# Key sums that stream the values of two heads at once, and extra transposes in other units

## Chip, cores and metric

One core of one Trainium2 chip runs the whole program, in one launch. The metric is the device time in microseconds (us) of one execution. TensorE is called PE below, VectorE DVE, ScalarE ACT, GpSimdE POOL and the queue that issues most DMAs SP, as the profile calls them.

## What is computed

The inputs are fp32. Three stages follow each other: a linear attention with random features over 2 batches of 8 heads, 576 tokens and 64 dimensions, then two mixtures of experts on the 1152 resulting tokens. Only the first stage is touched by the change:

```python
def phi(x):
    proj = np.einsum('bhsd,md->bhsm', x, omega)          # 128 features
    sq = np.sum(x * x, axis=-1, keepdims=True) / 2.0
    h = proj - sq
    h = h - np.max(h, axis=-1, keepdims=True)
    return np.exp(h) / np.sqrt(m)
q_p, k_p = (phi(q_s), phi(k_s))
kv = np.einsum('bhsm,bhsd->bhmd', k_p, v)                # the sums over keys
z = np.sum(k_p, axis=2)
num = np.einsum('bhsm,bhmd->bhsd', q_p, kv)
den = np.einsum('bhsm,bhm->bhs', q_p, z)[..., None] + 1e-06
return (num / den).astype(np.float32)
```

Then `_moe_ref` sums four experts, weighted by given probabilities, and `_moe2_ref` sends each token to one of eight experts.

## The kernel before

The attention is cut into **units**, and each unit goes through stages: `stage_a` transposes its rows of K or Q on PE (tile `tp`) and ACT copies the result out (`xt`, L181); `stage_b` projects on omega on PE (`pj`, L194), then DVE takes the maximum over features (L203), POOL or DVE subtracts and adds the square term (L206, L207, tile `sh`), DVE subtracts it from the projections (L209) and ACT takes the exponential (L210), which leaves the features `phk`, `pht` or `phq`. The squares themselves come from ACT (`sqt`, L168), a DVE reduction (L169) and a small POOL instruction (`sq`, L170).

A unit of K is one head of one head pair of one batch, 512 keys of it. Below, K20 is head pair 2, head 0. Two more units, T0 and T1, hold the last 64 keys of all heads, for heads 0 to 3 and 4 to 7. The order of units in batch 0 is K00, K01, K10, T0, K11, T1, K20, K21, K30, K31; then come Q0 to Q3 (one per head pair), four more units of Q, the units of K and Q of batch 1, and the tails of Q. The last stage of a unit of K is `c`: four matmuls with the features as weights and the values of this head as the moving operand (64 columns and a column of ones: 65), and a fifth for the tail, all summed in one PSUM tile `kvp`, of which DVE copies the 65 columns to `kvall` (L229). The values of both heads of a pair lie in one tile `v`, loaded by two DMAs.

A unit of Q goes on with `c` (transposes of the features, `tpq`), `d` (products with `kvall`, `nm`, and the division on DVE) and `e`.

Each fp32 matmul has two records in the trace, so the ten matmuls of two units of K are twenty records.

The table `WARM` names units by the order of their `stage_a`, from 0: in those the first transpose is made again that many times, into the same place, without effect on the result.

From 17 us on, the weights of the first expert layer come in (`r`, 512 KB each) and are split for it: ACT copies halves to a rounded form (`wf`, L497 and L500) and POOL takes the remainders (L499 and L501). Apart from a few stretches that are written out by hand, a scheduler sets the order of the instructions on each engine when the kernel is built, from costs of its own; on the chip each of ACT, DVE, POOL and SP then works through its list in that order.

Of the kernel before, what the change touches and what calls it, by code (L numbers as in the profile page):

```python
# [18 lines left out]
def perf_moe_kernel(  # L19
# [15 lines left out]
    nc = tc.nc  # L35
    P = 128
    B, H, S, D = q.shape
# [14 lines left out]
    FILL = {20: 1, 22: 1, 27: 3, 31: 2, 32: 1, 33: 1, 35: 1, 41: 1, 43: 1, 45: 1, 47: 1, 51: 2, 53: 1, 55: 1}  # L52
    NEA = 6
    SHV = range(10, 20)
    WARM = {10: 3, 13: 3}
    MS = 2
    XT = 2
    XL = 2
# [53 lines left out]
    def attention(att):  # L112
# [7 lines left out]
        T = {}  # L120
        ps = {}

        def bank(shape, name):
            tag, bufs = "a", 4
            if ps["wide"]:
                tag, bufs = (("a", 4), ("h", 2), ("a", 4), ("o", 2))[ps["n"] % 4]
                ps["n"] += 1
            return (ps["A"] if tag == "a" else psB).tile(shape, F32, tag=tag, bufs=bufs, name=name)
# [36 lines left out]
        def squares(src, name):  # L165
            t = att.tile([P, 8, D], F32, tag="sqt", bufs=1, name="sqt")
            s = att.tile([P, 8, 1], F32, tag="sq", bufs=4, name="sq")
            nc.scalar.activation(t, src, AF.Square)  # L168
            nc.vector.tensor_reduce(s, t, axis=AX.X, op=ALU.add)  # L169
            nc.gpsimd.tensor_scalar(s, s, 0.5 * scale, None, op0=ALU.mult)  # L170
            T["sq", name] = s

        def stage_a(u):
            tp = bank([P, 2 * P], "tp")

            for i in (0,) * WARM.get(ps["u"], 0) + (0, 1):
                nc.tensor.transpose(tp[:, i * P : (i + 1) * P], u["src"](i), ident)  # L177
            ps["u"] += 1
            xt = att.tile([P, 2 * P], F32, tag="xt", bufs=4, name="xt")
            if ps["u"] <= R0:  # L180
                nc.scalar.copy(xt, tp)  # L181
                u["terms"] = ((xt, omBD),)
            else:
                xh = xt.bitcast(F32R)
                xl = att.tile([P, 2 * P], F32R, tag="xl", bufs=XL, name="xl")
                nc.scalar.copy(xh, tp)
                nc.vector.tensor_tensor(xl, tp, xt, op=ALU.subtract)
                u["terms"] = ((xh, omH), (xh, omL), (xl, omH))

        def stage_b(u, tag, bufs):  # L190
            pj = bank([P, 4, M], "pj")
            for i in range(2):
                for n, (x, o) in enumerate(u["terms"]):
                    nc.tensor.matmul(  # L194
                        pj[:, 2 * i : 2 * i + 2, :],
                        x[:, i * P : (i + 1) * P],
                        o,
                        start=(n == 0),
                        stop=(n == len(u["terms"]) - 1),
                    )  # L200
            sh = att.tile([P, 4], F32, tag="sh", bufs=4, name="sh")
            sq = u["sq"]()
            nc.vector.tensor_reduce(sh, pj, axis=AX.X, op=ALU.max)  # L203
            ps["m"] = ps.get("m", -1) + 1
            eng = nc.vector if ps["m"] in SHV else nc.gpsimd
            eng.tensor_tensor(u["shv"](sh), u["shv"](sh), sq, op=ALU.subtract)  # L206
            eng.tensor_tensor(u["shv"](sh), u["shv"](sh), sq, op=ALU.add)  # L207
            ph = att.tile([P, 4, M], F32, tag=tag, bufs=bufs, name=tag)
            nc.vector.tensor_tensor(ph, pj, sh.unsqueeze(2).to_broadcast([P, 4, M]), op=ALU.subtract)  # L209
            nc.scalar.activation(ph, ph, AF.Exp, scale=scale)  # L210
            u["ph"] = ph

        def k_unit(b, hp, h):
            u = dict(
                src=lambda i: T["k", b, hp][:, h, 2 * i : 2 * i + 2, :],
                sq=lambda: T["sq", ("k", b, hp)][:, 4 * h : 4 * h + 4, 0],
                shv=lambda s: s,
            )

            def c():  # L220
                kvp = bank([P, D + 1], "kvp")
                hh = 2 * hp + h
                vt = T["v", b, hp]
                rows = slice(64 * b, 64 * b + 64)
                kpt = T["kpt", hh // 4]
                for j in range(4):
                    nc.tensor.matmul(kvp, u["ph"][:, j, :], vt[:, h, j, :], start=(j == 0), stop=False)  # L227
                nc.tensor.matmul(kvp, kpt[rows, hh % 4, :], T["vt"][rows, hh, :], start=False, stop=True)  # L228
                nc.vector.tensor_copy(kvall[:, b, hh, :], kvp)  # L229

            def a():
                stage_a(u)
                if h == 0:
                    squares(T["k", b, hp].rearrange("p h j d -> p (h j) d"), ("k", b, hp))

            def kb():
                kp = bank([P, 2, M], "kp")
                for i in range(2):
                    nc.tensor.transpose(kp[:, i, :], kvall[:, b, 2 * hp + i, D : D + 1].to_broadcast([P, P]), ident)
                t = att.tile([P, 2, M], F32, tag="kb", bufs=KBB, name=f"kb_{b}_{hp}")  # L240
                nc.scalar.copy(t, kp)
                T["kb", b, hp] = t

            T["mk", b, hp] = kb
            return [a, lambda: stage_b(u, "phk", 5), lambda: None, c]
# [1360 lines left out]
```

## Time and profile before

| | |
|---|---|
| median of three executions | 564.35 us (560.31, 564.35, 569.29) |
| the profiled execution | 565.68 us, its span 564.0 us |
| PE busy | 545.0 us, 97% of the span |
| mean granted clock of PE | 0.987 of 2.4 GHz |
| attention, units of K and Q | to about 136 us |

The span runs from the first to the last instruction; what lies around it is 1.68 us. The granted clock of PE is shown as a share of 2.4 GHz, so that 0.50 is 1.2 GHz. A weight load of PE (PEld) can overlap the matmuls ahead of it.

### The profile page before, as it was taken

How to read it: one execution, taken by the hardware profiler on the slowest of the kernel's cores; microseconds unless marked ns; L12 is line 12 of the kernel's file. 1: busy time of each engine (PE TensorE's matmuls, PEld its weight loads, DVE VectorE, ACT ScalarE, POOL GpSimd, SP SyncE). 2: the span in 40 equal slices, each digit the busy share in tenths (PEclk: the TensorE clock that was granted, in tenths of full speed). 3: DMA queues.
4: the chain of work that ended last, by engine and by line, in shares of the span. 5: the costliest groups of instructions: out<-in, count | busy, mean ns of one | idle time of the engine just before them, and what ended most of it. 6: DMA issues, size and time to landing. Idle time of an engine off the chain costs nothing.

```text
span 564.0 us, 10501 instructions
## 1 busy us (share of the span) xinstructions
PE 545.0 (97%) x4110; PEld 482.6 (86%) x4110; DVE 311.5 (55%) x747; ACT 210.9 (37%) x470; POOL 169.1 (30%) x267
## 2 busy tenths in 40 slices
PE   7898999999999999999999999999999999999894
PEld 5787999887999889999898999898998898888673
DVE  5748877996213368677557678556313314436130
ACT  5558445753112255454444455353112212211100
POOL 3356111102998225334332344003000000113332
PEclk9959999999999999999999999999999999999999
DMA  9945300000000322242222332322002089979910
GB/s 196 276 116 165 113 20 2 0 2 2 1 1 0 129 71 101 85 133 83 74 76 76 103 122 76 136 83 83 0 1 112 2 318 389 328 245 334 369 20 10
DMA packets 53046, 62.76 MB, mean 111 GB/s; under 512 B 15762, under 2 KB 32762, under 8 KB 52992
## 3 DMA queue, kind: packets, MB, share of 16 engines
q1 hardware_dynamic: 50016, 60.34, 32.1%
q0 software_dynamic: 1648, 1.38, 1.2%
q8 instruction: 33, 0.54, 0.4%
q10 hardware_dynamic: 1328, 0.33, 0.3%
q14 instruction: 21, 0.17, 0.1%
HBM read 58.30 MB, written 4.46 MB: 111 GB/s over the span
## 4 chain that ended last, share of the span: by engine, by line
PE 94%; DVE 2%; issue 1%; POOL 1%; DMA 1%; ACT 0%; POOLq 0%; DVEq 0%; ACTq 0%
PE h L512 18%; PE o L533 18%; PE o L691 18%; PE X L634 9%; PE Y L634 7%; PE pj L194 6%; PE kvp L227 3%; PE yps L1351 2%; PE m L1330 2%; PE tp L177 1%; PE gl L989 1%; PE nm L343 1%; PE kvp L228 1%; PE nm L351 1%; PE tpq L314 1%
## 5 line engine op out<-in xcount | busy, mean ns | idle before, releaser
L533 PE MATMUL o<-wf,hhi 128*128 128x512 f32 x288 | 91.8, 399 | 0.0
L691 PE MATMUL o<-w2f,sh 128*128 128x512 f32 x288 | 89.9, 393 | 0.0
L512 PE MATMUL h<-xfar,wf 128*128 128x256 f32 (+1 forms) x480 | 81.4, 310 | 0.0
L512 PEld LDWEIGHTS h<-xfar,wf 128*128 128x128 f32 x480 | 71.9, 188 | 2.7 <-issue 0.4
L523 DVE SCALAR_TENSOR_TENSOR hlo<-h,hhi 128x384 fp32r<-128x384 f32 (+1 forms) x56 | 27.9, 498 | 79.2 <-ACT hhi L522 79.1
L522 ACT ACTIVATE hhi<-h 128x384 fp32r<-128x384 f32 (+1 forms) x56 | 25.0, 446 | 112.5 <-PE h L512 109.0
L533 PEld LDWEIGHTS o<-wf,hhi 128*128 128x128 f32 x288 | 51.5, 189 | 7.5 <-ACT hhi L522 0.3
L533 PE MATMUL o<-wf,hlo 128*128 128x512 f32 x144 | 57.3, 399 | 0.0
L691 PEld LDWEIGHTS o<-w2f,sh 128*128 128x128 f32 x288 | 50.9, 188 | 7.0
L691 PE MATMUL o<-w2f,sl 128*128 128x512 f32 x144 | 56.2, 390 | 0.0
L597 POOL TENSOR_TENSOR sums<-r 128x256 f32<-128x256 f32 x16 | 18.6, 1160 | 110.2 <-DVE ws L610 91.9
L512 PE MATMUL h<-xnear,wf 128*128 128x384 f32 x192 | 37.3, 341 | 0.0
L512 PEld LDWEIGHTS h<-xnear,wf 128*128 128x128 f32 x192 | 33.7, 188 | 1.1
L533 PEld LDWEIGHTS o<-wf,hlo 128*128 128x128 f32 x144 | 27.0, 188 | 6.1 <-DVE hlo L523 0.3
L691 PEld LDWEIGHTS o<-w2f,sl 128*128 128x128 f32 x144 | 27.1, 188 | 6.1
L634 PEld LDWEIGHTS X<-tf,ws 128*128 128x128 f32 x192 | 28.9, 188 | 3.0 <-ACT p L655 0.3
L634 PE MATMUL X<-tf,ws 128*128 128x256 f32 (+1 forms) x192 | 30.8, 295 | 0.0
L1075 POOL TENSOR_SCALAR nmx<-mx 128x1 f32<-128x1 f32 x9 | 2.0, 219 | 93.5 <-DVE act L1001 93.4
L203 DVE TENSOR_REDUCE sh<-pj 128x4 f32<-128x512 f32 x36 | 24.7, 688 | 9.3 <-PE pj L194 9.0
L645 ACT ACTIVATE sh<-p 128x256 fp32r<-128x256 f32 (+1 forms) x32 | 14.2, 444 | 40.1 <-DVE p L669 36.2
L613 DVE TENSOR_TENSOR w2f<-r,w2f 128x1024 fp32r<-128x1024 f32 x16 | 20.8, 1302 | 9.0 <-ACT w2f L611 9.0
L194 PE MATMUL pj<-omBD,xt 128*128 128x256 f32 x72 | 23.6, 468 | 2.1 <-DVE phq L209 1.3
(302 smaller groups left out, 1083.9 us busy)
## 6 DMA issues: line engine op xcount, KB each, us to landing
r<-in_moe_w_dram SPq DMA_DIRECT2D x48, 512.0 KB, 4.4
vw<-in_moe_w_dram SPq DMA_DIRECT2D x20, 1024.0 KB, 9.4
xs_far<-in_moe_w_dram SPq DMA_DIRECT2D x3, 1024.0 KB, 15.0
k<-in_k_dram SPq DMA_DIRECT2D x8, 256.0 KB, 3.5
v<-in_v_dram SPq DMA_DIRECT2D x16, 128.0 KB, 3.2
q<-in_q_dram SPq DMA_DIRECT2D x8, 256.0 KB, 4.3
xrow<-xacc SPq DMA_DIRECT2D x6, 256.0 KB, 5.9
out_dram<-xacc SPq DMA_DIRECT2D x6, 256.0 KB, 5.8
```

The source lines that it names most:

```text
L194: nc.tensor.matmul(pj[:, 2 * i : 2 * i + 2, :], x[:, i * P : (i + 1) * P], o, start=(n == 0), stop=(n == len(u["terms"]) - 1),)
L203: nc.vector.tensor_reduce(sh, pj, axis=AX.X, op=ALU.max)
L227: nc.tensor.matmul(kvp, u["ph"][:, j, :], vt[:, h, j, :], start=(j == 0), stop=False)
L512: nc.tensor.matmul(ph[:, 0:n], wf[:, a, c * P : (c + 1) * P], xx[:, c, :], start=(idx == 0), stop=(idx == 3 * NC - 1),)
L522: nc.scalar.activation(hh[:, 0:n], ph[:, 0:n], AF.Relu)
L523: nc.vector.scalar_tensor_tensor(hl[:, 0:n], ph[:, 0:n], 0.0, hh[:, 0:n].bitcast(F32), op0=ALU.max, op1=ALU.subtract)
L533: lambda idx=idx, a=a, hx=hx: nc.tensor.matmul(outs[t], hx[:, cs], wf[:, a, :], start=(f == 0 and idx == 0), stop=(f == NF - 1 and idx == 2))
L597: G.tensor_tensor(raw(0), quad(1, 0), quad(1, 1), op=ALU.add)
L613: V.tensor_tensor(w2f[:, 1], r2, w2f[:, 0].bitcast(F32), op=ALU.subtract)
L634: nc.tensor.matmul(o, w[a][:, c, :], x[b][:, c, :], start=(start and t == c == 0), stop=(t == 2 and c == 1), skip_group_check=True,)
L645: A.activation(hh[i][:, cs], src, AF.Relu)
L691: nc.tensor.matmul(outs[t], hx[i][:, lo : lo + P], w2f[:, a, i, :], start=(fp == 0 and idx == 0), stop=(fp == NF // 2 - 1 and idx == 5),)
```

## The change

In `c` of a unit of K the moving operand is now the values of both heads of the pair, 130 columns, and PSUM takes a tile of that width; of it DVE copies the 65 columns of this unit's head as before. The other 65 columns are not used. `WARM` changes from three extra transposes in unit 10 (Q0) and three in unit 13 (Q3) to two in unit 9 (K31) and two in unit 13.

```diff
-    WARM = {10: 3, 13: 3}
+    WARM = {9: 2, 13: 2}
...
             def c():
-                kvp = bank([P, D + 1], "kvp")
+                kvw = bank([P, 2, D + 1], "kvp")
+                kvp = kvw[:, h, :]
                 hh = 2 * hp + h
+
                 vt = T["v", b, hp]
                 rows = slice(64 * b, 64 * b + 64)
                 kpt = T["kpt", hh // 4]
                 for j in range(4):
-                    nc.tensor.matmul(kvp, u["ph"][:, j, :], vt[:, h, j, :], start=(j == 0), stop=False)
-                nc.tensor.matmul(kvp, kpt[rows, hh % 4, :], T["vt"][rows, hh, :], start=False, stop=True)
+                    nc.tensor.matmul(kvw, u["ph"][:, j, :], vt[:, :, j, :], start=(j == 0), stop=False)
+                nc.tensor.matmul(
+                    kvw, kpt[rows, hh % 4, :], T["vt"][rows, 2 * hp : 2 * hp + 2, :], start=False, stop=True
+                )
                 nc.vector.tensor_copy(kvall[:, b, hh, :], kvp)
```

The scheduler gives the engines another order with it, from about 14 us of the program to the end of the attention; behind that the lists of all engines are the same as before. Lines below the edit have numbers higher by four. Three places follow.

ACT, from the features of T0 (`pht_186`) to those of K20; the tile `pht_247` holds the features of T1, `xt x2` are K21 and K30, and `wf_0`, `wf_1` are the first weights. Before:

```order
L210 ACTIVATE pht_186<-pht_186 128x512
L181 COPY xt<-tp 128x256
L210 ACTIVATE phk<-phk 128x512
L210 ACTIVATE pht_247<-pht_247 128x512
L181 COPY xt<-tp 128x256 x2
L168 ACTIVATE sqt<-k_3_289 128x512
L497 CAST wf_0_703<-r_0_700 128x512
L497 CAST wf_1_708<-r_0_700 128x512
L168 ACTIVATE sqt<-q_0_359 128x512
L210 ACTIVATE phk<-phk 128x512
```

The same stretch of ACT now:

```order
L210 ACTIVATE pht_186<-pht_186 128x512
L210 ACTIVATE phk<-phk 128x512
L168 ACTIVATE sqt<-k_3_289 128x512
L181 COPY xt<-tp 128x256
L168 ACTIVATE sqt<-q_0_361 128x512
L501 CAST wf_0_701<-r_0_698 128x512
L501 CAST wf_1_706<-r_0_698 128x512
L168 ACTIVATE sqt<-q_1_390 128x512
L210 ACTIVATE pht_247<-pht_247 128x512
L181 COPY xt<-tp 128x256 x2
L504 CAST wf_0_701<-r_0_698 128x512
L168 ACTIVATE sqt<-q_2_419 128x512
```

The two copies of weights and the squares of Q0 and Q1 have moved from behind T1's exponential and the copies `xt` of K21 and K30 to ahead of them.

DVE at the same place, from the maximum of T1 to the features of K20 (the last row). Before:

```order
L203 TENSOR_REDUCE sh<-pj 128x4
L229 COPY kv<-kvp 128x65 x3
L209 TENSOR_TENSOR pht_247<-pj,sh 128x512
L101 TENSOR_REDUCE psm<-praw 128x9
L169 TENSOR_REDUCE sq<-sqt 128x8
L102 TENSOR_SCALAR psm<-psm 128x9
L229 COPY kv<-kvp 128x65
L103 RECIPROCAL psm<-psm 128x9
L203 TENSOR_REDUCE sh<-pj 128x4
L104 TENSOR_TENSOR pn<-praw,psm 128x36
L169 TENSOR_REDUCE sq<-sqt 128x8
L209 TENSOR_TENSOR phk<-pj,sh 128x512
```

The rows of DVE now, between the same two:

```order
L203 TENSOR_REDUCE sh<-pj 128x4
L103 RECIPROCAL psm<-psm 128x9
L169 TENSOR_REDUCE sq<-sqt 128x8
L209 TENSOR_TENSOR pht_247<-pj,sh 128x512
L104 TENSOR_TENSOR pn<-praw,psm 128x36
L233 COPY kv<-kvp 128x65
L203 TENSOR_REDUCE sh<-pj 128x4
L169 TENSOR_REDUCE sq<-sqt 128x8
L209 TENSOR_TENSOR phk<-pj,sh 128x512
```

The square sums of Q1 and Q2 (the two rows of L169) now stand ahead of the subtractions for T1 and for K20.

POOL, around the square term of K31 (the last L206 and L207 of each piece). Before:

```order
L206 TENSOR_TENSOR sh<-sh,sq 128x4
L207 TENSOR_TENSOR sh<-sh,sq 128x4
L170 TENSOR_SCALAR sq<-sq 128x8
L143 MEMSET v_1_776 128x8
L206 TENSOR_TENSOR sh<-sh,sq 128x4
L207 TENSOR_TENSOR sh<-sh,sq 128x4
L501 TENSOR_TENSOR wf_0_703<-r_0_700,wf_0_703 128x512
```

The same place of POOL now:

```order
L170 TENSOR_SCALAR sq<-sq 128x8
L143 MEMSET v_1_774 128x8
L503 TENSOR_TENSOR wf_2_714<-r_1_711,wf_2_714 128x512
L505 TENSOR_TENSOR wf_2_714<-r_1_711,wf_2_714 128x512
L206 TENSOR_TENSOR sh<-sh,sq 128x4
L503 TENSOR_TENSOR wf_3_833<-r_1_711,wf_3_833 128x512
L207 TENSOR_TENSOR sh<-sh,sq 128x4
```

Three remainders of weights now stand ahead of the second of the two small instructions. On SP, the loads of the first K of batch 1 and of the first half of `r` have moved ahead of the two loads of `v_3`, and stand right behind the four loads of Q.

## Rows read from the trace of the kernel before

**Rows 1.** The page: engines' busy time, granted clock in 40 slices, chain by engine.
```profile
PE 545.0 (97%) x4110; PEld 482.6 (86%) x4110; DVE 311.5 (55%) x747; ACT 210.9 (37%) x470; POOL 169.1 (30%) x267
...
PEclk9959999999999999999999999999999999999999
...
PE 94%; DVE 2%; issue 1%; POOL 1%; DMA 1%; ACT 0%; POOLq 0%; DVEq 0%; ACTq 0%
```

**Rows 2.** Stretches: length, busy time and count by engine, clock, DMA share, GB/s.
```profile
14.00:20.00 6.00, 6.00 (x43) 5.33 (x43) 4.74 (x13) 2.44 (x5) 1.36 (x8) 1.00 0.94 272
20.00:26.80 6.80, 5.37 (x33) 4.24 (x31) 4.59 (x9) 4.33 (x10) 3.81 (x9) 1.00 0.98 301
26.80:40.50 13.70, 13.70 (x48) 11.80 (x47) 6.76 (x15) 7.60 (x16) 7.65 (x13) 0.50 0.35 89
40.50:56.00 15.50, 13.61 (x100) 12.04 (x99) 13.53 (x37) 12.66 (x27) 9.41 (x9) 1.00 0.60 193
56.00:100.00 44.00, 44.00 (x334) 41.47 (x333) 34.74 (x98) 21.57 (x50) 7.25 (x27) 1.00 0.14 43
```

**Rows 3.** Timeline of PE: start, length of the run, instruction, idle before.
```profile
20.75 1.99 PE L194 MATMUL pj<-omBD,xt 128*128 128x256 f32 x8 [0.30 <-ACT xt L181]
22.58 0.71 PE L177 MATMUL tp<-ident,q 128*128 128x128 f32 x5
23.96 1.08 PE L227 MATMUL kvp<-v,phk 128*128 128x65 f32 x8 [0.67 <-POOL wf L499]
...
35.13 1.81 PE L227 MATMUL kvp<-v,phk 128*128 128x65 f32 x8
...
40.78 0.60 PE L269 MATMUL tpq<-ident,phq 128*128 128x128 f32 x4
...
42.05 1.10 PE L343 MATMUL nm<-kv,qT 128*128 128x65 f32 x8
42.99 1.08 PE L194 MATMUL pj<-omBD,xt 128*128 128x256 f32 x4
```

**Rows 4.** Timeline of PE's weight loads, for the second `kvp` of rows 3.
```profile
23.93 0.97 PEld L227 LDWEIGHTS kvp<-v,phk 128*128 128x128 f32 x8 [0.88 <-POOL wf L499]
```

**Rows 5.** Timeline of ACT.
```profile
20.32 0.65 ACT L181 COPY xt<-tp 128x256 f32<-128x256 f32 x2 [1.12 <-PE tp L177]
20.86 0.64 ACT L168 ACTIVATE sqt<-k 128x512 f32<-128x512 f32 x1
21.67 1.14 ACT L497 CAST wf<-r 128x512 fp32r<-128x512 f32 x2 [0.17 <-DMA r<-in_moe_w_dram]
...
23.25 0.61 ACT L210 ACTIVATE phk<-phk 128x512 f32<-128x512 f32 x1
```

**Rows 6.** Timeline of DVE.
```profile
21.53 0.69 DVE L169 TENSOR_REDUCE sq<-sqt 128x8 f32<-128x512 f32 x1 [0.69 <-ACT sqt L168]
...
22.73 1.28 DVE L203 TENSOR_REDUCE sh<-pj 128x4 f32<-128x512 f32 x2
25.48 0.69 DVE L209 TENSOR_TENSOR phk<-pj,sh 128x512 f32<-128x512 f32 x1 [1.47 <-POOL sh L207]
```

**Rows 7.** Timeline of POOL.
```profile
22.31 0.23 POOL L170 TENSOR_SCALAR sq<-sq 128x8 f32<-128x8 f32 x1 [0.94 <-DVE sq L169]
22.50 2.50 POOL L499 TENSOR_TENSOR wf<-r,wf 128x512 fp32r<-128x512 f32 x2
24.96 0.21 POOL L206 TENSOR_TENSOR sh<-sh,sq 128x4 f32<-128x4 f32 x1
```

**Rows 8.** Timeline of the DMA queue SP: when issues began, and how long they took.
```profile
11.24 2.00 SPq L149 DMA_DIRECT2D q<-in_q_dram  x4
...
16.13 0.56 SPq L149 DMA_DIRECT2D k<-in_k_dram  x1
16.74 0.47 SPq L486 DMA_DIRECT2D r<-in_moe_w_dram  x1
```

**Rows 9.** The page: DMA issues, KB each, median time to landing.
```profile
r<-in_moe_w_dram SPq DMA_DIRECT2D x48, 512.0 KB, 4.4
```

## Prediction

> **What bounds the kernel now.** I read the page first: PE is busy for 97% of the span and 94% of the chain that ended last is PE, so a change counts by what it does to PE's time: its work, its waits and its clock. The 40 slices of the granted clock show one loss, a slice at half speed near the start [rows 1]. A table by stretches places it: from 26.8 to 40.5 us the clock is 0.50, 1.2 GHz, and PE is busy for all 13.70 us; in the 6.8 us ahead of it the clock was full and PE was busy for only 5.37 us [rows 2]. At half clock PE is the bound: DVE and ACT work for 6.76 and 7.60 us in that stretch. At full clock PE's work there would take some 6.85 us, so 6.85 us is the most that a kept clock could give. From 40.5 to 56 us PE waits for 1.89 us of 15.5, with DVE and ACT busy for 13.53 and 12.66; from 56 to 100 us PE never waits [rows 2].
>
> The change lies in these stretches. Whoever reads the diff alone sees wider matmuls and one transpose more or less; the lists of the engines show that the larger part is a new order, and it has to be costed on ACT, DVE and POOL, which the wide matmuls don't touch.
>
> **Columns.** 160 records (16 units of K, ten records each) stream 130 columns and not 65. Eight records of 65 columns take 1.08 us, 0.135 each, and their eight weight loads 0.97 us, 0.12 each [rows 3, 4]: the load of 128x128 weights sets the pace, not the columns. For 130 columns the trace has no row. The nearest are transposes, of 128 columns: a run of five took 0.71 us and one of four 0.60, so one more costs 0.11 us, no more than a weight load. On the other side four records of 256 columns took 1.08 us, 0.27 each; on a line from 65 to 256 columns a record of 130 gains 0.045 us [rows 3]. The 80 records of batch 0 lie where PE waits anyway; the 80 of batch 1 lie in the stretch where it never does. So 0 to 3.6 us; a saving is excluded, since no instruction becomes shorter. I take 0, by the transposes, which are much the nearest.
>
> The Trainium skill weighs against the change here: TensorE: Matmul & The Clock Gate, section "Back-to-back issue gap", gives the start-to-start time of a warm matmul as its columns divided by 2.4 GHz plus 2.5 ns, by which (an estimate) 65 more columns add 27 ns, 2.2 us for the 80 records, and the sum below would be 569.5. The row of 128 columns speaks for the other reading, and no row of before settles it for 130.
>
> The second head's values are in the same tile, and their DMA was issued right behind the first's; no unit waits longer for them that I can see.
>
> **Transposes.** The three that go from Q0 (0.33 us at 0.11) stood ahead of a `kvp` for which PE then waited 0.67 us [rows 3]: gain 0. The two in K31 stand ahead of another `kvp` that must wait for its features (below): cost 0. One fewer in Q3 is 0.1 us. The sum of these is at most 0.3 us either way; I take 0.
>
> **The new order.** Before, ACT copied `xt` of K21 and K30 at 20.32 us and then, at 21.67, reached the first copy of weights, for which it waited on the DMA [rows 5]. Now that copy, a second one and the squares of Q0 and Q1 stand ahead of the `xt`. When does the first `r` land? It is issued right behind the four loads of Q (11.24 and 2.00 long) and one of K (0.56), at 13.8, not at 16.74 [rows 8]. At the median of 4.4 us to landing [rows 9] it is there at 18.2. But the DMA engines are busy for 94% from 14 to 20 us, at 272 GB/s [rows 2]; what really leaves the queue ahead of it are two loads of V, 256 KB, 0.96 us at that rate, so it lands at 20.7 by that reading. I take 20.0, nearer to the full queue.
>
> From there, at the durations of [rows 5 to 7] (a copy of weights 0.57, squares 0.64, square sum 0.69, maximum 0.64, subtraction 0.69, exponential 0.61, `xt` 0.33, a remainder on POOL 1.25, its two small ones 0.25 each, `sq` 0.23), each step waits for the one ahead of it on its engine or for its data:
>
> First, two copies, squares of Q1, then DVE's square sum, which now stands ahead of T1's subtraction, then that subtraction, T1's exponential and `xt`: 20.0 + 1.14 + 0.64 + 0.69 + 0.69 + 0.61 + 0.33 = 24.1. The projections of K21 and K30 start then, not at 20.75 [rows 3]. Second, the other `xt`, a copy, squares of Q2, their sum on DVE (ahead of K20's subtraction), subtraction, exponential: 24.1 + 0.33 + 0.57 + 0.64 + 0.69 + 0.69 + 0.61 = 27.6 for the `kvp` of K20, before 23.96. Third, from K20's subtraction at 27.0: POOL has `sq` from 26.3, a remainder, K21's two small ones, a remainder and K30's two, to 30.0; K30's subtraction and exponential to 31.3; `xt` of Q0 and squares of Q3 to 32.3; their sum to 33.0; then POOL's `sq`, two remainders, a small one, a third remainder and the other small one of K31: 33.0 + 0.23 + 2.5 + 0.25 + 1.25 + 0.25 = 37.5; subtraction and exponential: 38.8 for the `kvp` of K31, before 35.13 [rows 3]. Fourth, `xt` and squares on ACT, the square sum, four small DVE instructions and a maximum between them, Q0's subtraction and exponential: 38.8 + 0.33 + 0.64 + 0.69 + 0.75 + 0.64 + 0.69 + 0.61 = 43.2 for the first `tpq`, before 40.78.
>
> So the units of K end 2.4 us later, **with full clock throughout**: the 6.85 us that the clock gives back are eaten by new waits, some 3.7 us ahead of 24.1, 1.5 ahead of 27.6 and 3 ahead of 38.8. With the landing at 18.2 or 20.7 it is +0.6 or +3.1.
>
> **The clock.** The row of before shows it falling behind a stretch with 1.4 us of waits in 6.8. The new order has a longer wait, so I expect a fall here too, and perhaps a second one at 38.8. At half clock eight `kvp` records take 1.81 us for 1.08 [rows 3], but most of that lies beside the chain on ACT, DVE and POOL. Bounds: 0, if all is hidden, and 6.85, half of another stretch like the old one. I take 1.5, near the low end, since PE has over 8 us of waits there to hide it.
>
> **What comes back.** Eleven of the sixteen copies of weights now stand ahead of the first `qT` on ACT, before seven: 4 x 0.57 = 2.3 us leave ACT in the next stretch. There PE waits for 1.89 us in all [rows 2], so 0 to 1.9; DVE, the busier one, isn't relieved: I take 1.0.
>
> **Sum.** 565.7 (the profiled execution) + 2.4 + 1.5 - 1.0 = 568.6. That execution was 1.3 us above the median of 564.35, so 567.3, rounded to **567 us**. Own range of this case: 564 to 571, by the landing (-1.8, +0.7), the clock (-1.5, +2.5) and what comes back (-0.9, +1).
>
> **Rivals.** (1) The clock holds, and PE stays the bound: the waits of my chain are shorter than I make them (the landing early, POOL and ACT a little ahead), wide `kvp` keep PE at 2.4 GHz. Then the stretch of 13.7 us shrinks, at best to ACT's 7.60: 565.7 - 6.1 = 559.6, less 1.3: 558. For it: PE had no idle time in that stretch. Against it: the lists above. Chance 0.27.
>
> (2) Slower: the clock falls a second time, at the wait ahead of K31's `kvp`, and stays at 1.2 GHz through the first units of Q for as long as before, 13.7 us. PE is busy for 13.61 of 15.5 us there at full clock, so of the 6.85 us lost only 1.89 find room: +5.0, 573.6 with the rest of my sum less 1.3, 572. It decides as soon as the granted clock reads 0.50 for over 8 us behind 40 us; with a third fall it passes 576. For it: fewer expert matmuls fill PE among the first units of Q now. Against it: these units kept the clock before, with PE waiting for 1.89 us [rows 2]. Chance 0.15.
>
> (3) Columns are paid by their number: + 3.6 us in batch 1, 571. For it the 256 columns of rows 3, against it the transposes. Chance 0.1. The rule of the Trainium skill's section named above (TensorE: Matmul & The Clock Gate, "Back-to-back issue gap") would be this rival at 2.2 us.
>
> **How the numbers follow.** My case 0.48, rival 1 0.27, rival 2 0.15, rival 3 0.1. The executions of before differ by 9 us, so a median of a few is itself uncertain by 2 us or so. Low 557: rival 1, 558, and half of that; high 574: rival 2, 572, and that. Outside lie a part of rival 1 (0.1) and of rival 2 (0.07), under 0.2. A difference under 2% (11.3 us) can hardly be told from none here: faster than 553 would need more than all of the 6.85 us, 0.03; slower than 576 needs rival 2 with more, 0.07; within, 0.9.
>
> **What would show it.** Right: PE waits for over 2 us ahead of the projections of K21; ACT's copy of weights waits on the DMA until about 20 us and stands ahead of `xt`; the first `tpq` at 42 to 45 us; eight `kvp` records of 130 columns still at about 1.08 us; the granted clock 0.50 somewhere from 23 to 31 us. Wrong: the first `tpq` ahead of 40 us and the clock at 1.00 throughout (rival 1); or `kvp` records 0.04 us longer where PE never waits (rival 3). What would upset all of it is the phase of the clock's falls, which the three executions of before, 9 us apart, may already reflect.

## The result, and the profile after

The changed kernel takes **566.49 us** (median of 21 executions, 564.89 to 570.21), the kernel before, beside it on the same chips, 563.60 (21 executions, 558.94 to 569.29). The ratio is 1.0064 with a 95% interval from 1.0042 to 1.0085: no difference at a bound of 2%, a small loss by the interval. The profiled execution took 567.01 us, its span 565.3. The ratios here and below leave out executions more than 1.5% longer than the fastest of the same kernel (three of ten in the run no_split_before below), so they are not the quotients of the medians.

The page of the changed kernel, PE's row and the granted clock in 40 slices:

```profile
PE 542.3 (96%) x4108; PEld 477.9 (85%) x4108; DVE 312.8 (55%) x747; ACT 211.8 (37%) x470; POOL 168.0 (30%) x267
...
PEclk9899999999999999999999999999999999999999
```

Against [rows 1], PE has 2.7 us less work in the trace (less of it at half clock), but the span is 1.3 us longer. The same stretches as in [rows 2], of the changed kernel:

```profile
14.00:20.00 6.00, 6.00 (x43) 5.15 (x42) 5.63 (x14) 3.16 (x6) 1.75 (x10) 1.00 0.99 305
20.00:26.80 6.80, 3.82 (x14) 2.94 (x13) 3.24 (x7) 4.61 (x10) 4.54 (x8) 0.75 1.12 321
26.80:40.50 13.70, 12.29 (x73) 9.66 (x73) 8.55 (x19) 8.64 (x18) 9.41 (x17) 1.00 0.51 142
40.50:56.00 15.50, 13.25 (x100) 11.73 (x99) 13.97 (x37) 11.78 (x25) 8.66 (x8) 1.00 0.52 154
56.00:100.00 44.00, 44.00 (x326) 40.29 (x325) 34.66 (x98) 21.33 (x46) 5.33 (x26) 1.00 0.12 36
```

The stretch at half clock from 26.8 to 40.5 us is gone (0.50 to 1.00): the clock is at 1.2 GHz only from 23.3 to 26.7 us. In its place PE waits, for 2.98 + 1.41 + 2.25 = 6.64 us from 20 to 56 us; in [rows 2] it was 1.43 + 0 + 1.89 = 3.32. Where PE waits, its timeline shows (start, length, instruction, idle before):

```profile
23.86 3.40 PE L194 MATMUL pj<-omBD,xt 128*128 128x256 f32 x8 [2.98 <-ACT xt L181]
...
27.31 1.06 PE L229 MATMUL kvp<-v,phk 128*128 128x130 f32 x8
...
37.17 1.16 PE L229 MATMUL kvp<-v,phk 128*128 128x130 f32 x8 [1.06 <-ACT phk L210]
...
39.92 0.66 PE L273 MATMUL tpq<-ident,phq 128*128 128x128 f32 x4
```

These are the four places of the chain in the prediction (24.1, 27.6, 38.8 and 43.2 there; 20.75, 23.96, 35.13 and 40.78 in [rows 3]). ACT's timeline shows where the first wait comes from:

```profile
21.36 1.14 ACT L501 CAST wf<-r 128x512 fp32r<-128x512 f32 x2 [2.36 <-DMA r<-in_moe_w_dram]
22.41 0.62 ACT L168 ACTIVATE sqt<-q 128x512 f32<-128x512 f32 x1
22.94 0.61 ACT L210 ACTIVATE pht<-pht 128x512 f32<-128x512 f32 x1
23.46 0.62 ACT L181 COPY xt<-tp 128x256 f32<-128x256 f32 x2
```

The copies stand ahead of `xt` and wait 2.36 us for `r`, against 0.17 us in [rows 5], where `xt` had gone ahead of them.

Something that I had not foreseen stands in DVE's timeline, in its small instructions (L206, L207; 128x4 elements), and beside them in POOL's, in the remainders:

```profile
39.16 1.02 DVE L207 TENSOR_TENSOR sh<-sh,sq 128x4 f32<-128x4 f32 x1
...
41.54 1.10 DVE L206 TENSOR_TENSOR sh<-sh,sq 128x4 f32<-128x4 f32 x1
42.68 0.16 DVE L207 TENSOR_TENSOR sh<-sh,sq 128x4 f32<-128x4 f32 x1
...
46.15 1.20 DVE L207 TENSOR_TENSOR sh<-sh,sq 128x4 f32<-128x4 f32 x1
```

```profile
38.90 2.50 POOL L503 TENSOR_TENSOR wf<-r,wf 128x512 fp32r<-128x512 f32 x2 [0.39 <-ACT wf L501]
...
41.36 1.27 POOL L505 TENSOR_TENSOR wf<-r,wf 128x512 fp32r<-128x512 f32 x1
...
46.05 2.63 POOL L503 TENSOR_TENSOR wf<-r,wf 128x512 fp32r<-128x512 f32 x2
```

The one at 42.68 takes 0.16 us with POOL idle; the three others begin just behind the start of a remainder and end with one (40.18 and 40.15; 42.64 and 42.63; 47.35 and, at half of the run's 2.63 us, 47.37). Four of them take over 0.3 us (the fourth, at 45.66, ends with a remainder too), 3.78 us together; from 40.5 to 56 us, where three of them lie, DVE is busier than PE (13.97 us against 13.25).

### The profile page after: what moved, and what is told of

The parts are those of the page before. It is cut to its first block, busy times and chain, and to the rows that moved or that the text cites. A ratio compares the mean times of both kernels' runs of the same rounds, so it can differ in the third digit from the quotient of the medians.

```text
span 565.3 us, 10491 instructions
## 1 busy us (share of the span) xinstructions
PE 542.3 (96%) x4108; PEld 477.9 (85%) x4108; DVE 312.8 (55%) x747; ACT 211.8 (37%) x470; POOL 168.0 (30%) x267
## 3 DMA queue, kind: packets, MB, share of 16 engines
q0 software_dynamic: 1648, 1.38, 1.2%
## 4 chain that ended last, share of the span: by engine, by line
PE 89%; DVE 3%; issue 2%; DMA 2%; POOL 2%; ACT 1%; SPq 0%; POOLq 0%; DVEq 0%
PE h L516 18%; PE o L537 18%; PE o L695 18%; PE X L638 9%; PE Y L638 7%; PE pj L194 4%; PE m L1334 2%; PE yps L1355 2%; PE gl L993 1%; PE kvp L229 1%; DMA r<-in_moe_w_dram 1%; PE tp L177 1%; PE nm L347 1%; PE nm L355 1%; PE tpq L318 1%
## 5 line engine op out<-in xcount | busy, mean ns | idle before, releaser
L516 PE MATMUL h<-xfar,wf 128*128 128x256 f32 (+1 forms) x480 | 80.1, 310 | 0.0
L601 POOL TENSOR_TENSOR sums<-r 128x256 f32<-128x256 f32 x16 | 18.2, 1138 | 111.0 <-DVE ws L614 92.0
L194 PE MATMUL pj<-omBD,xt 128*128 128x256 f32 x72 | 22.4, 447 | 3.6 <-ACT xt L181 3.2
```

The lines of the kernel that those rows point to most:

```text
L194: nc.tensor.matmul(pj[:, 2 * i : 2 * i + 2, :], x[:, i * P : (i + 1) * P], o, start=(n == 0), stop=(n == len(u["terms"]) - 1),)
L516: nc.tensor.matmul(ph[:, 0:n], wf[:, a, c * P : (c + 1) * P], xx[:, c, :], start=(idx == 0), stop=(idx == 3 * NC - 1),)
L601: G.tensor_tensor(raw(0), quad(1, 0), quad(1, 1), op=ALU.add)
```

## The experiments

Twelve runs in four groups; each group has executions of the kernel before on the same chip, the changed kernel itself was timed beside none of them, and so runs are compared by their ratios. No run has the wide sums in the order of before. "Last nm" is the start of the last run of `nm` in the profiled execution, the end of the attention on PE: 135.63 us in the first trace of before, 135.65 in that of after.

| run | us | before, same chip | ratio, 95% interval | first tpq | last nm |
|---|---|---|---|---|---|
| before_again | 564.84 | 565.85 | 0.9994, 0.9963 to 1.0026 | 34.5 | 130.84 |
| wait_filled | 569.85 | 565.85 | 1.0076, 1.0039 to 1.0113 | 39.8 | 135.32 |
| no_transposes | 570.62 | 565.85 | 1.0094, 1.0062 to 1.0125 | 39.4 | 135.11 |
| narrow_new_transposes | 571.77 | 565.85 | 1.0089, 1.0049 to 1.0129 | 41.7 | 137.30 |
| r_early | 569.88 | 565.14 | 1.0103, 1.0061 to 1.0145 | 35.9 | 135.35 |
| r_earlier | 569.20 | 565.14 | 1.0083, 1.0056 to 1.0110 | 39.7 | 136.56 |
| r_early_before | 567.25 | 565.14 | 1.0048, 1.0018 to 1.0079 | 37.2 | 132.06 |
| no_split_dve | 562.73 | 565.14 | 0.9967, 0.9938 to 0.9995 | 36.7 | 130.28 |
| no_split_before | 559.26 | 564.44 | 0.9907, 0.9877 to 0.9938 | 34.6 | 128.89 |
| no_split_early | 562.97 | 564.44 | 0.9971, 0.9949 to 0.9992 | 37.7 | 132.38 |
| write_only_pool | 563.11 | 564.44 | 0.9992, 0.9962 to 1.0023 | 36.9 | 133.67 |
| no_squares_before | 557.11 | 563.61 | 0.9875, 0.9836 to 0.9915 | 34.3 | 126.17 |

My theory at the start, **the order**: the lists of ACT, DVE and POOL, with `r`'s landing at their head, set the time of the changed kernel. Rival, **the clock**: how often PE falls to 1.2 GHz sets it, and waits only feed that.

**The kernel before, again** (no edit).

> The kernel before, unchanged, run against itself. Both theories: ratio 1.000 within 0.4%. What it tells apart is how its executions spread. Order theory: in the order of before PE is the bound between 26.8 and 40.5 us, so an execution is the longer the lower its mean granted clock is: 558 to 560 us at a mean clock of 0.995 and more, 564 to 569 at 0.985 to 0.988; the order of after does not follow its clock like that. Clock theory (the change acts through the clock and the columns alone): the executions of before and of after lie on one line of time against clock.

The median is the same, but the profiled execution isn't: its clock held through the attention (the page's row, and three of its stretches).

```profile
PEclk9999999999999999999999999999999999999998
```

```profile
20.00:26.80 6.80, 4.92 (x28) 3.99 (x28) 4.34 (x10) 4.23 (x10) 3.83 (x9) 1.00 1.01 305
26.80:40.50 13.70, 12.06 (x79) 10.13 (x78) 12.06 (x27) 10.65 (x22) 8.81 (x14) 1.00 0.53 155
40.50:56.00 15.50, 13.98 (x107) 13.04 (x108) 14.11 (x42) 12.68 (x29) 10.46 (x10) 1.00 0.54 156
```

Without the fall PE does 79 instructions from 26.8 to 40.5 us, not 48 [rows 2], and waits for 1.88 + 1.64 + 1.52 = 5.04 us from 20 to 56 us, not 3.32; the first `tpq` comes 6.3 us sooner and the attention ends 4.8 us sooner. So the fall is no property of the order of before: it comes in some executions. The trace I predicted from was one with a fall, and its last `nm` equals that of after by that accident. The mean granted clock of every execution tells how often, though not where in the kernel: of the 34 executions of before beside this group 17 stand at 0.990 or less (median 568.15 us) and 16 at 0.994 or more (562.79). Of the 21 of after none is below 0.991, and their times, 564.89 to 570.21, hardly follow the clock. That is the kind of spread that the theory of the order had, though at 0.995 and more it had before at 558 to 560 us.

**PE's long wait filled with transposes** (in the changed kernel, six more in K30, order otherwise unchanged).

```
-    WARM = {9: 2, 13: 2}
+    WARM = {8: 6, 9: 2, 13: 2}
```

> The changed kernel with six more transposes in the unit ahead of the long wait at 20.9 us (unit 8, K30); the lists of all engines are otherwise the same, row by row. Order theory: the wait ends when ACT's list ends it, at 23.9 us, whatever PE does in it; if the clock no longer falls at 23.3 us, the sums of K20 start at 26.6 and not at 27.3 us, so 0 to 1 us faster than after's 566.5. Clock theory: the fall is what the change costs; without it 2 us or more faster, or, if transposes don't keep the clock, no difference.

The clock no longer fell at 23 us; it fell at 38.0 instead, behind a wait of 1.75 us ahead of K31's `kvp`. The attention ends 0.3 us sooner than in after, and the time is that of the changed kernel within its interval. A clock kept at one wait was lost at a later one.

**No repeated transposes at all** (in the changed kernel).

```
-    WARM = {9: 2, 13: 2}
+    WARM = {}
```

> The changed kernel without any extra transposes; lists otherwise the same, row by row. Order theory: within 0.7 us of after (566.5), since the four transposes that go lay beside waits of PE (the clock may fall once more near 35 to 39 us, mostly beside the chain on ACT, DVE and POOL). Clock theory: the transposes are there for the clock, so a second stretch at half clock appears and costs 1.7 us or more: 568 to 570.

The fall is at 23.45 us as in after, the last `nm` 0.5 us sooner, and the time again that of the changed kernel. The moved transposes do nothing that can be seen here, where the interval is 1.8 us to either side.

**The new transposes alone** (65 columns; in the kernel before).

```
-    WARM = {10: 3, 13: 3}
+    WARM = {9: 2, 13: 2}
```

> The kernel before (65 columns) with only the new table of extra transposes. ACT's list stays that of before up to 28 us: the copies xt of K21 and K30 stand ahead of the weights. Order theory: the projections of K21 start at 20.5 to 21 us as before, and the time is that of before or better, 560 to 565 us, faster than after by 2 to 5 us. Clock theory: with narrow sums the clock falls at least as long as before, 13 us, and the time is 564 us or more.

Among the slowest of the first group, where the theory of the order had it fast. K21's projections stand at 21.07 us as before, but a copy of weights on ACT now stands ahead of K21's features, the clock fell for 10.2 us, and PE waits for 3.56 of the 15.5 us from 40.5. Two fewer transposes make the scheduler write lists that are as bad as those of the 130 columns, with sums of 65. The rival had the time (564 us or more), but from a fall of 13 us or more.

**`r` earlier** (in the changed kernel, loaded with K21; then with K20; then the first of these in the kernel before).

```
-                with_load(ku(2, 1), kl(3), vl(3)),
+                with_load(ku(2, 1), kl(3), vl(3), lambda: load_raw(0, 0)),
```

> The changed kernel with one edit: the first raw weights r are loaded with the loads of the unit K21, ahead of those of Q, and not behind them. Theory of the order (ACT's copies of weights, which now stand ahead of xt, wait for r's landing at 21.3 us, and everything behind follows): r lands at 16 to 18 us, the projections of K21 and K30 start at 20 to 21.5 us and not at 23.9, the first tpq comes 1.5 to 3 us ahead of 39.9, and the time is 2 to 4 us below the changed kernel's, 562 to 565 us on a chip like the first. Theory of the clock (PE's falls set the time, the landing only shifts waits): a fall comes somewhere else and the time is within 1 us of the changed kernel's, 566 to 568. Third way: r takes the place of q's loads in a full queue, q's land 1 us later and Q's units pay it back: 566 to 569.

> As the run above, with r loaded one unit sooner, with the loads of K20. Theory of the order: no further gain over the run above, since r at 15.7 us is there before ACT comes to its copies; 562 to 565 us. If the landing isn't what ACT waits for, both runs equal the changed kernel. If the queue of loads pays for it, this one is 0.5 to 1 us worse than the run above, since 128 KB now stand ahead of K21's loads too.

> The kernel before with the same edit as the first run of this call (65 columns, the old transposes, r loaded with the loads of K21). Theory of the order: in the kernel before ACT waits for r for little (its projections of K21 stand at 20.75 us, ahead of the copies), so an early r moves it by 0 to 1 us either way, 563 to 566 us, and by the new lists (copies ahead of features) perhaps 1 us up. Theory of the clock: what decides is how often the clock falls in the stretch behind 23 us; with PE's waits unchanged the executions stay in two groups some 6 us apart and the median stays where it is.

None is faster, and the theory of the order fails at its own test. In the first, `r` is there at 15.5 us and the first `tpq` comes 4.1 us sooner, but the projections of K21 don't (23.71), and the attention ends only 0.3 us sooner. At 23 us ACT's `xt` now waits for T1's features, which wait for T1's small instructions on POOL, which stand behind four remainders that an early `r` let in: another wait in the place of the one removed. And behind 40 us DVE gives the rest back. PE, DVE and POOL in that run:

```profile
23.71 1.99 PE L194 MATMUL pj<-omBD,xt 128*128 128x256 f32 x8 [1.39 <-ACT xt L181]
...
35.85 0.66 PE L273 MATMUL tpq<-ident,phq 128*128 128x128 f32 x4 [0.20 <-ACT phq L210]
...
52.10 1.13 PE L194 MATMUL pj<-omBD,xt 128*128 128x256 f32 x4 [1.38 <-DVE phq L209]
```

```profile
48.86 1.24 DVE L206 TENSOR_TENSOR sh<-sh,sq 128x4 f32<-128x4 f32 x1
50.14 1.18 DVE L207 TENSOR_TENSOR sh<-sh,sq 128x4 f32<-128x4 f32 x1
51.35 0.69 DVE L209 TENSOR_TENSOR phq<-pj,sh 128x512 f32<-128x512 f32 x1
```

```profile
48.81 2.49 POOL L505 TENSOR_TENSOR wf<-r,wf 128x512 fp32r<-128x512 f32 x2 [0.58 <-ACT wf L504]
```

Two remainders end at 50.05 and 51.30; DVE's two small instructions, 0.3 us of work, end at 50.10 and 51.32, and PE's projections wait 1.38 us for what stands behind them. Six such took 5.58 us in this run. The clock held throughout, so the rival, the clock, doesn't explain it either. In the kernel before an early `r` cost a little.

**A third theory: DVE held by POOL.** Without DVE's two small instructions for the units Q0 to Q3 and the other units on DVE (a rounding step of the shift is left out), in the changed kernel:

```
-            eng.tensor_tensor(u["shv"](sh), u["shv"](sh), sq, op=ALU.subtract)
-            eng.tensor_tensor(u["shv"](sh), u["shv"](sh), sq, op=ALU.add)
+            if ps["m"] not in SHV:
+                eng.tensor_tensor(u["shv"](sh), u["shv"](sh), sq, op=ALU.subtract)
+                eng.tensor_tensor(u["shv"](sh), u["shv"](sh), sq, op=ALU.add)
```

> The changed kernel without the two small DVE instructions (subtract sq and add it back) for those units whose squares go through DVE; this leaves a rounding step out of the features' shift. Theory of the collision (those instructions, some 0.15 us long, took 1.0 to 1.2 us where they lay beside a remainder on POOL, four times between 39 and 46.5 us, 3 us in all, and DVE is the engine that is late there): the stretch from 40 to 56 us gets 1.5 to 3 us shorter and the time falls to 563 to 565 us on a chip like the first. Rival (the long ones only fill waits of DVE, which is late for POOL's sq anyway): only the 0.15 us each of those on the path go, 0 to 0.6 us, 565.5 to 567.

562.73 us, just below the 563 to 565 expected, and PE's waits from 40.5 to 56 us, 2.25 us in after, are gone:

```profile
40.50:56.00 15.50, 15.50 (x124) 14.66 (x123) 13.09 (x33) 11.88 (x28) 8.12 (x7) 1.00 0.62 197
```

The attention ends 5.4 us sooner, more than the 3.8 us that the four long ones took. But 3.25 us of that are won by the first `tpq` (36.67 for 39.92), which waits for a subtraction on DVE (38.43 in after) that stands ahead of the first long one (39.16): that part belongs to the lists, which changed too. From the first `tpq` to the last `nm` it is 93.6 us against 95.7. So this run leaves 2.1 us for the place and doesn't show the mechanism. The next one tests that: all of DVE's small instructions stay, and POOL's remainders become fills that write as many places and read none (the low parts of the first expert layer's weights are left out).

```
-        eng.tensor_tensor(l1, s1, d1.bitcast(F32), op=ALU.subtract)
+        eng.tensor_tensor(l1, s1, d1.bitcast(F32), op=ALU.subtract) if e else eng.memset(wf[:, 1, :].bitcast(F32), 0.0)
...
```

> The changed kernel with POOL's remainders of the first expert layer's weights replaced by a fill with zeros, which writes the same 128x512 places but reads nothing; the low parts of those weights are left out, and POOL no longer waits for ACT's copies. DVE's two small instructions are all there. Theory of the port (DVE's small instruction has two inputs in SBUF, and is held until a POOL instruction that reads SBUF is done): all of them take 0.15 to 0.2 us, also beside a fill, and the waits of PE behind 40 us shrink: 561 to 564 us. Rival (DVE is slowed by any POOL work beside it, or by what waits for its semaphores): some still take 0.5 to 1.2 us and the time stays at 565 to 568.

All occurrences of the two instructions, in the changed kernel and then in this run (count, shortest, median and longest ns, first and last start):

```profile
L206 DVE TENSOR_TENSOR sh<-sh,sq x10: 151/152/1102, 37.6 to 66.8; 128x4 f32<-128x4 f32 x10
L207 DVE TENSOR_TENSOR sh<-sh,sq x10: 150/153/1197, 38.2 to 67.2; 128x4 f32<-128x4 f32 x10
```

```profile
L206 DVE TENSOR_TENSOR sh<-sh,sq x10: 151/152/163, 34.6 to 64.3; 128x4 f32<-128x4 f32 x10
L207 DVE TENSOR_TENSOR sh<-sh,sq x10: 134/161/165, 34.8 to 64.7; 128x4 f32<-128x4 f32 x10
```

The longest is 0.165 us, and two of the twenty lay beside a fill and were over before it was:

```profile
39.86 0.52 POOL L505 MEMSET wf<- 128x512 f32 x1
40.09 0.15 DVE L206 TENSOR_TENSOR sh<-sh,sq 128x4 f32<-128x4 f32 x1
40.31 0.13 DVE L207 TENSOR_TENSOR sh<-sh,sq 128x4 f32<-128x4 f32 x1
```

So, as far as two go, it takes a POOL instruction that reads. A rule of the Trainium skill says what these rows show (SBUF — State Buffer, section "Who interferes with whom"): a VectorE instruction with two inputs in SBUF contends with a GpSimd instruction that reads SBUF, not with one that only writes. The same section of the Trainium skill says that the order of issue decides which of the two is blocked; each of the four long ones in after began behind the POOL instruction that it ended with. L206 and L207 have both inputs in SBUF; the subtraction L209 has one in PSUM, and its 0.69 us are the same everywhere.

The time is another matter. The theory's range of 561 to 564 us holds the 563.11, but not for its reason: PE's waits behind 40 us were to shrink, and they stayed at 2.21 us (2.25 in after):

```profile
40.50:56.00 15.50, 13.29 (x99) 11.96 (x98) 13.41 (x38) 11.87 (x25) 0.70 (x3) 1.00 0.57 169
```

From the first `tpq` to the last `nm` it is 96.7 us here and 95.7 in after. What was won was won ahead of the first `tpq` (36.9 for 39.9 us): the fills are shorter (0.53 us against 1.27), and K31's two small instructions, which stand behind them on POOL, come at 31.8 and 32.4 us and not at 34.2 and 35.5. This run shows what holds DVE's instructions, and not that the holding costs the kernel time.

**The same instructions left out of the kernel before, and with an early `r`** (edits as above).

> The kernel before without DVE's two small instructions for the units whose squares go through DVE (the same rounding step left out as in the run without them on the changed kernel; 65 columns, the old transposes). Theory of the collision (these instructions, when they lie beside a remainder on POOL, make up what tells the two kernels apart once r has landed): with none left in either, the two are within 1 us of each other, here 561 to 564 us on a chip like the last. Rival (the order of before is the better one in itself, since its projections of K21 don't wait for r): 3 us or more below the changed kernel without them, 557 to 560 us. Third way (clock): two groups again, some 6 us apart, the lower one at 557 to 560.

> The changed kernel without DVE's two small instructions and with r loaded with the loads of K21. Theory of the collision (it ate what the early r had won, 4.1 us at the first tpq and 0.3 at the end of the attention): now the early r keeps what it wins, but PE has no wait left behind 40 us, so only PE's wait ahead of K21's projections (2.05 us in the run without the small instructions) can go: 1 to 2 us below that run, 560.5 to 562. Rival (an early r costs elsewhere, in the queue of q's loads): the same as that run or 1 us more, 562.5 to 564.

Two misses of the third theory, which had the two kernels within 1 us of each other. 559.26 us is 3.5 us below the changed kernel without them (0.9907 against 0.9967). Part of the 3.5 is the clock, as their mean clocks show: 20 of the 27 executions of before in this group stand at 0.988 or less, four of the ten of this run, none of the twelve of no_split_dve. Between executions at 0.995 or more this run is 2.1 us below before (558.79 against 560.88) and no_split_dve 0.3 us (562.31 against 562.59).

The profiled executions show where the rest lies. Beside before_again the attention ends 1.95 us sooner, none of it won by the first `tpq` (34.6 for 34.5); from there on it is 94.3 us against 96.4, 2.1 us less, as in the changed kernel (93.6 against 95.7). By these two pairs these instructions, with their own 0.15 us each and with what they were held, cost both kernels about the same behind the first `tpq`, some 2 us; that can hide what an earlier stage wins, but isn't what tells the two apart. That lies ahead of the first `tpq`: 5.4 us between before_again and after, 2.1 between the two runs without these instructions.

And an early `r` again won nothing (562.97); its profiled execution had the clock at 1.2 GHz from 18.2 to 25.0 us.

**The kernel before without square terms** (they cancel but for rounding; squares, sums, small instructions and that rounding are left out).

```
         def squares(src, name):
-            t = att.tile([P, 8, D], F32, tag="sqt", bufs=1, name="sqt")
...
+            pass
...
-            eng.tensor_tensor(u["shv"](sh), u["shv"](sh), sq, op=ALU.subtract)
-            eng.tensor_tensor(u["shv"](sh), u["shv"](sh), sq, op=ALU.add)
```

> The kernel before without the square terms at all: no squares on ACT, no square sums on DVE, no small instructions on DVE or POOL that subtract them from the maximum and add them back (they cancel but for rounding, which is left out). Theory (the chain over ACT, DVE and POOL is what PE waits for ahead of 56 us, some 2.7 us in the run of the kernel before without DVE's small instructions): most of these waits go, 1 to 2.5 us below that run, and an execution at a lower mean clock is rarer since PE waits less; 556 to 558 us on a chip like the last. Rival (the waits are for loads and copies of weights, which stay, and the scheduler's new lists bring others): 558.5 to 562 us.

```profile
20.00:26.80 6.80, 6.50 (x44) 5.63 (x43) 5.02 (x13) 3.87 (x8) 2.61 (x3) 1.00 0.73 227
26.80:40.50 13.70, 13.70 (x97) 12.43 (x96) 9.22 (x21) 10.68 (x24) 8.51 (x9) 1.00 0.77 229
40.50:56.00 15.50, 15.50 (x128) 14.93 (x127) 13.13 (x34) 11.96 (x28) 9.15 (x8) 1.00 0.71 224
```

The fastest of all, 557.11 us, where the theory of the chain had 556 to 558, and the steadiest (556.40 to 558.13): PE waits for 0.3 us from 20 to 56, and no execution's mean clock is below 0.996.

## Why the prediction was right, and where its steps failed

The time (567 for 566.49) and "no difference" were right, and most of the picture: PE waits ahead of K21's projections for the landing of `r`, one fall of the clock in 23 to 31 us, the gain from the old fall eaten by waits. Several sizes were wrong and cancelled, and that the time agrees to 0.5 us is luck in good part.

**Columns: taken as 0, measured 0.86 us in batch 1 and up to 1.7 in all.** At full clock, where PE never waits, a `kvp` of batch 1 in after, and one in the second trace of before:

```profile
74.48 1.06 PE L229 MATMUL kvp<-v,phk 128*128 128x130 f32 x8
75.47 0.49 PE L230 MATMUL kvp<-vt,pht 64*128 64x130 f32 x2
75.88 0.39 PE L194 MATMUL pj<-omH,xt 128*128 128x256 f32 x1
```

```profile
70.22 1.00 PE L227 MATMUL kvp<-v,phk 128*128 128x65 f32 x8
71.16 0.43 PE L228 MATMUL kvp<-vt,pht 64*128 64x65 f32 x2
71.52 0.39 PE L194 MATMUL pj<-omH,xt 128*128 128x256 f32 x1
```

From the first start to that of the next work it is 1.40 us against 1.30. Over the eight units of batch 1, from unrounded starts, the price is 0.054 us for the eight records and 0.054 for the two: 0.108 us a unit, 0.86 us for batch 1 and as much for batch 0 where PE is not waiting. It comes once per run of records and not per record, so the weight load does set the pace within a run, as I argued, and rival 3's 3.6 us are out. The formula that I weighed there (the Trainium skill, TensorE: Matmul & The Clock Gate, "Back-to-back issue gap") would make it 2.2 us in batch 1, an estimate; the trace gives 0.86. The same section says that the formula is a lone matmul's and that in a stream of weight loads and matmuls both set the pace, and that part the trace bears out.

**Transposes: 0, right.** Without any, or with six more, the time stays within the intervals.

**The new order: +2.4, measured -0.9 at the first `tpq`.** Of the four places 24.1 and 27.6 were met (23.86, 27.31), the first by two errors that cancel: `r` landed at 21.3 us, not 20.0, and the square sum of Q1, which I put ahead of T1's subtraction, ran behind it (23.07): the sum that stands ahead is Q0's, and both were done by 20.3, before `r` came. The two sums that I called Q1's and Q2's when I listed DVE's rows are thus Q0's and Q1's. The second place was met by luck too: K20's features were done at 26.6 us, and PE, at half clock until 26.7, came to them at 27.3.

```profile
19.04 0.69 DVE L169 TENSOR_REDUCE sq<-sqt 128x8 f32<-128x512 f32 x1 [0.17 <-ACT sqt L168]
19.64 0.68 DVE L209 TENSOR_TENSOR pht<-pj,sh 128x512 f32<-128x512 f32 x1
...
23.07 0.69 DVE L169 TENSOR_REDUCE sq<-sqt 128x8 f32<-128x512 f32 x1 [1.90 <-ACT sqt L168]
...
29.65 0.68 DVE L169 TENSOR_REDUCE sq<-sqt 128x8 f32<-128x512 f32 x1
...
36.97 0.67 DVE L169 TENSOR_REDUCE sq<-sqt 128x8 f32<-128x512 f32 x1
```

The step that failed is the last two: 38.8 was 37.17, and 43.2 was 39.92. In the third I let POOL wait for Q3's square sum, to 33.0 us; the one that it waits for is again a unit earlier, Q2's, done at 30.3, and 0.99 us of waiting for ACT's copies took back a part. In the fourth I put Q0's square sum, maximum and small steps behind K31's exponential; on the chip a square sum (36.97) and the maxima (36.37, 37.63) ran beside it or right behind. I had called a first `tpq` of 42 to 45 us the sign of my case; at 39.92 it came just ahead of the 40 us that I named for rival 1, whose other half, a held clock, didn't come.

**The clock: +1.5, measured 1.4.** PE was busy for 2.87 us of the 3.4 at 1.2 GHz, half of which is lost. What I missed is the base: I read the 13.65 us at half clock as part of the kernel, and it is part of some executions. The second fall of rival 2 didn't come: from 26.8 us on the stretches of after stand at 1.00.

**What comes back: -1.0, wrong in sign.** PE's waits from 40.5 to 56 us grew from 1.89 to 2.25 us. I asked only how much ACT was relieved; three of the four waits in that stretch, 1.64 of the 2.25 us, are for DVE, whose instructions were held beside POOL there.

The account of the two profiled executions: waits 6.64 - 3.32 = +3.3; half clock (13.65 - 2.87) / 2 = -5.4; columns +1.7; two transposes fewer, 0.11 each, -0.2. That makes -0.6, where the layer behind the attention ends 0.4 us later; a remainder of about 1 us I can't place. The last 0.9 us of the 1.3 come behind 514 us, where the change has no part that I know of.

Against the second trace of before, in which the clock held, the same account makes +1.6 for waits, +1.4 for the clock and +1.5 for columns and transposes: 4.5 of the 4.8 us between the ends of the attention. So the change costs some 4.8 us against an execution of before whose clock holds, and nothing there against one whose clock falls; the medians, 2.9 us apart, lie between. The 3.5 us between the two kernels without DVE's small instructions are made in the same way: 1.8 us are left between executions at a mean clock of 0.995 or more, and 1.4 between the ends of the attention in their profiled ones. What stays open is what decides, in an execution of one and the same kernel, whether the clock falls, and how the 5.4 us at the first `tpq` part between the wide sums and the order, since no run has the wide sums in the order of before; by the price above, eight units' sums are 0.86 us of them at most.

## What to carry to other kernels

Before a sum is made from one profiled execution, take a second one: a stretch at half clock may belong to the execution, and then the base of the sum, not only its terms, is off. An edit that feeds a scheduler should be costed by the lists that it writes, and a wait removed at the head of such lists can be worth nothing: here DVE was late behind it, and with DVE's small instructions left out an early `r` won nothing either. Look for short instructions whose longest occurrence is many times their median, and at what ran beside those; but an instruction that is held costs the kernel only what a later wait of PE shows.

## What the runs showed of the hardware

A DVE instruction of 128x4 elements with both inputs in SBUF takes 0.15 us alone and up to 1.25 us (L207 in before_again) beside a POOL instruction that reads SBUF, ending with it; two that lay beside one that only writes took 0.15 and 0.13 us. Ten records of 130 columns in runs of eight and two cost 0.108 us more than of 65, by the run and not by the record. The same kernel's clock fell for 13.65 us in one profiled execution and not at all in the attention of another, 4.8 us apart at its end.
